# Windowed attention and a maxout layer on one core: scores of a batch's first chunk packed into six PSUM banks, the sinks' v product moved, one cast moved

## The chip, the cores and the metric

The kernel runs on one core of a Trainium2 chip. The metric is the device time of one execution in microseconds (us). All inputs come from the chip's memory (HBM) in float32, and the float32 output goes back there. Inside, the products run on bfloat16 with float32 sums.

The engines go by the names of the profile: PE is TensorE (PEld its weight loads), DVE is VectorE, ACT is ScalarE, POOL is GpSimd, SP is SyncE, which issues most transfers. Each engine takes its instructions strictly in the order in which the program emits them, and waits where the next one's operands or its buffer aren't ready.

## The reference

Two steps follow each other: an attention with a window and four sink positions, for 4 batches, 8 heads, 768 positions and a head size of 64; and a feed-forward layer whose hidden value is the larger of three products.

```python
scores = scale * np.matmul(q, k.transpose(0, 1, 3, 2))
is_sink = pos[None, :] < int(n_sink)             # n_sink = 4
in_window = (rel >= 0) & (rel < int(window))     # rel = query - key, window = 128
scores = np.where(is_sink | in_window, scores, -1000000000.0)
a = np.exp(scores - np.max(scores, axis=-1, keepdims=True))
a = a / (np.sum(a, axis=-1, keepdims=True) + 1e-09)
attn = np.matmul(a, v)
x = attn.transpose(0, 2, 1, 3).reshape(B * S, H * D)      # 3072 x 512
h = np.maximum(np.maximum(x @ w1, x @ w2), x @ w3)        # 512 -> 768
out = h @ w_out                                           # 768 -> 512
```

## The kernel before

**Tiling.** A batch's 768 positions are three *chunks* of 256, so there are twelve chunks, 0 to 11 (`NCH`), three to a batch (`CPB`). A chunk has two blocks of 128 queries, and its 8 heads are four *pairs* (`NP`): a = 0 and 1 are the two heads of a pair, whose 64 rows of head size lie on the upper and lower half of the 128 partitions, so that two matmuls of 64 rows stand side by side in TensorE.

**Scores.** `score(ci, pairs)` (L263) makes, transposed (keys on partitions), the score blocks that the window reaches. They have slots s of 128 columns in one bank of PSUM per head: s = 0 is the previous chunk's second key block against the first query block, s = 1 and 2 (one matmul of 256 columns) the chunk's first key block against both query blocks, s = 3 the second key block against the second. A batch's first chunk (ci % 3 == 0) has no previous one, so its slot 0 is empty: per head a matmul of 256 and one of 128 columns, in a bank of which three quarters are used. `expo` (L286) takes the exponential on ScalarE, one instruction per head (512 columns, or 384 in a first chunk); `mask` (L293) multiplies the pair by a 0/1 mask on VectorE (`msk`, in first chunks `msk0`; 1024 or 768 columns).

**Sinks.** The four sink positions lie in a batch's first chunk. `sink_k` (L229, GpSimd) gathers their keys, `sink_v` (L314) their values by eight small matmuls with a selection matrix (output `sv`), which VectorE copies to `vs`. Chunks 1 and 2 of a batch use them: `sink_score` (L298) makes the sink scores `sk`, ScalarE their exponential `e_sink`, and `av_open` (L328) starts the output `o` with the product of `e_sink` and `vs`. `av(ci, p)` (L343) then adds the window's blocks for one pair; VectorE takes the reciprocal `rc` of the sum of weights and writes `x_sb`.

**Feed-forward.** `xpose` (by TensorE and a copy) or `xpose_dma` (L379, by a DMA transpose on the SP queue) turns `x_sb` into `xT`. `ffn_h(ci, fp, wi)` (L386) multiplies by a third of the columns of w1, w2 or w3 (eight matmuls of 256 columns into one bank `h_ps`); for w1 ScalarE copies the result to `h_sb`, for the other two VectorE takes the maximum with it (L405). `ffn_y(ci, t)` (L409) makes one of a chunk's two output blocks from `h_sb` (six matmuls of 512 columns, `y_ps`), which ScalarE or VectorE copies to `y_sb` (L417).

**Stages.** From chunk 4 on a loop (L666) runs one stage per chunk n = i + 1: its attention, `ffn_y` of chunk i − 1 and `ffn_h` of chunk i, so each stage starts with scores, two `ffn_y`, then nine `ffn_h` with the four `av` between. The order within a stage is written out by hand: one for n = 4 (L668), one for the last two, one for the second and third chunks of a batch (L766: 5, 7, 8, 10) and one for the first chunks (L809: 6 and 9). In a stage for a first chunk the scores of pairs 0, 3 and 1 come before the two `ffn_y`, those of pair 2 after them. Before the loop chunks 0 to 3 have an order of their own; the part with chunk 3 ends at L660.

**Banks and queues.** PSUM has eight banks, which `bank()` hands out first in, first out, in the order of the program: a bank that was given back last comes last. The loads of q, k and v of chunk i + 3 and the transposes of kT, qT and xT are on the SP queue, in the order of the program. GpSimd makes most casts to bfloat16: `cast_qk` (L95) and `cast_v` (L105), the latter in four quarters per chunk.

Of the kernel before, what the change touches and what calls it, by code (L numbers as in the profile page):

```python
# [9 lines left out]
F32 = mybir.dt.float32  # L10
BF16 = mybir.dt.bfloat16
AF = mybir.ActivationFunctionType
# [4 lines left out]
def kernel(  # L17
# [13 lines left out]
    nc = tc.nc  # L31
# [8 lines left out]
    scale = 1.0 / (D ** 0.5)  # L40
    NP = H // 2
    CPB = S // 256
# [6 lines left out]
    with tc.manual_schedule():  # L49
        const = tc.alloc_tile_pool(name="const", bufs=1)  # L50
        raw = tc.alloc_tile_pool(name="raw", bufs=2)
        work = tc.alloc_tile_pool(name="work", bufs=2)
# [4 lines left out]
        def bank(shape, dtype, name):  # L57
            j = free.pop(0)
            x = psum.tile(shape, dtype, tag=f"b{j}", name=name)
            home[id(x)] = x, j  # L60
            return x

        def give(*banks):
            for x in banks:
                free.append(home.pop(id(x))[1])

        RING = 4
# [37 lines left out]
        def cast_v(ci, n, i, eng):  # L105
            if ci >= NCH:
                return
            eng.tensor_copy(  # L108
                vb[ci % RING][64 * i:64 * i + 64, n, :, 0:D],
                raws[ci, "v"][64 * n:64 * n + 64, :, i])  # L110

# [99 lines left out]
        def masks_late():  # L211
            for a in range(2):
                nc.gpsimd.tensor_scalar(msk[:, a], addm, 2.0 ** -30, 1.0, op0=ALU.mult, op1=ALU.add)
            for a in range(2):
                nc.gpsimd.tensor_scalar(msk0[:, a], addm0, 2.0 ** -30, 1.0, op0=ALU.mult, op1=ALU.add)

        sel = const.tile([128, 2, 32], BF16, name="sel")

        def sink_init():
# [43 lines left out]
        def score(ci, pairs):  # L263
# [3 lines left out]
            for p in pairs:  # L267
# [15 lines left out]
                e = work.tile([128, 2, 4, 128], BF16, tag="e", bufs=2 * NP, name="e_sb")  # L283
                es[ci, p] = e, st

        def expo(ci, p):  # L286
            lo = 0 if ci % CPB else 1
            e, st = es[ci, p]
            for a in range(2):
                nc.scalar.activation(e[:, a, lo:], st[a][:, lo:], AF.Exp, scale=scale)  # L290
                give(st[a])

        def mask(ci, p, eng=None):  # L293
            lo = 0 if ci % CPB else 1
            e = es[ci, p][0]
            (eng or nc.vector).tensor_mul(e[:, :, lo:], e[:, :, lo:], msk0 if lo else msk)  # L296
# [17 lines left out]
        def sink_v(b):  # L314

            x = vb[(b * CPB) % RING]
            sv = bank([128, 2, D + 1], F32, "sv")
            for a in range(2):
                for p in range(NP):
                    nc.tensor.matmul(  # L320
                        sv[32 * p:32 * p + 32, a], lhsT=sel[:, a], rhs=x[:, 0, 2 * p + a],
                        start=True, stop=True, tile_position=(0, 32 * p))
            nc.vector.tensor_copy(vs[b % 2], sv)
            give(sv)
# [18 lines left out]
        def av(ci, p):  # L343
            b, c = divmod(ci, CPB)
            o = os_[ci, p]
            e = es[ci, p][0]
            first = c == 0
            for t in range(2):
                for a in range(2):
                    blocks = [(1, ci, 0)] if t == 0 else [(2, ci, 0), (3, ci, 1)]  # L350
                    if t == 0 and c:
                        blocks = [(0, ci - 1, 1)] + blocks
                    for s, cv, n in blocks:
                        nc.tensor.matmul(  # L354
                            o[:, t, a], lhsT=e[:, a, s], rhs=vb[cv % RING][:, n, 2 * p + a],
                            start=first, stop=True, skip_group_check=True)
                        first = False
            rc = work.tile([128, 2, 2], F32, tag="rc", bufs=4, name="rc")
            nc.vector.reciprocal(rc, o[:, :, :, D])  # L359
            if ci not in xs:  # L360
                xs[ci] = work.tile([128, 2, NP, 2, D], BF16, tag="x", bufs=2, name="x_sb")
            nc.vector.tensor_mul(xs[ci][:, :, p], o[:, :, :, 0:D],  # L362
                                 rc.unsqueeze(3).to_broadcast([128, 2, 2, D]))
            give(o)
# [280 lines left out]
        load(5, 'v', gate=after(0))  # L645
        ffn_h(2, 0, 2)
        av(3, 0)
        cast_v(4, 0, 1, nc.vector)
        cast_v(4, 1, 0, nc.gpsimd)
        load(5, 'q')  # L650
        av(3, 2)
# [9 lines left out]
        def sinks(n):  # L661
            if n % CPB == 1:
                sink_k(n // CPB)
                sink_v(n // CPB)

        for i in range(3, NCH):  # L666
            n, m = i + 1, i - 1
            if i == 3:  # L668
# [17 lines left out]
                mask(n, 1)  # L686
                expo(n, 2)
                mask(n, 0)
                sink_score(n)
                ffn_h(i, 0, 0)  # L690
                expo(n, 3)
# [74 lines left out]
            elif n % CPB:  # L766
                load(i + 3)
                sink_score(n)
                score(n, (0,))
                expo(n, 0)  # L770
                score(n, (3,))
# [36 lines left out]
                ffn_h(i, 2, 2, 1 if i + 2 < NCH else 2)  # L808
            else:  # L809
                sink_k(n // CPB)  # L810
                sink_v(n // CPB)
                load(i + 3)
                score(n, (0,))
                expo(n, 0)
                score(n, (3,))
                score(n, (1,))
                expo(n, 1)
                expo(n, 3)
                ffn_y(m, 0, nc.vector)
                mask(n, 0)  # L820
                ffn_y(m, 1)
                score(n, (2,))
                mask(n, 3)
                av_open(n)
                mask(n, 1)
                expo(n, 2)
                av(n, 0)
                mask(n, 2)
                ffn_h(i, 1, 0)
                ffn_h(i, 0, 0)  # L830
                av(n, 1)
# [64 lines left out]
```

## Time and profile before

| | before |
|---|---|
| three runs, us | 178.89 to 179.43, median 179.43 |
| profiled execution, us | 179.04 |
| its span, first to last instruction, us | 177.3 |
| mean granted TensorE clock | 0.996 |
| busy, us: PE | 170.1 |
| busy, us: DVE | 126.5 |
| busy, us: ACT | 85.8 |
| busy, us: POOL | 67.1 |

A row of the timeline shows the start of a group of like instructions in us from the start of the span, its length, engine, line, operation, `output<-input`, the shape and the count; in brackets stands how long the engine had been idle before, and what ended that. Matmuls are pipelined: one of 128 columns shows a duration of some 0.2 us, but the next one starts long before its end, so the places of TensorE are read by starts. A row of a table by stretches has the stretch, its length, the busy time (and the count of instructions), the granted clock, the busy share of the DMA engines and GB/s.

### The profile page before, as it was taken

What the parts mean: (1) busy time and instruction counts of PE and PEld (TensorE: products, weight loads), DVE (VectorE), ACT (ScalarE), POOL (GpSimd) and SP (SyncE); (2) the same over time, 40 slices, a digit from 0 to 9 for tenths busy, and PEclk for the clock granted to TensorE, in tenths of its full rate; (3) what the DMA queues carried; (4) which work ended last, traced back from release to release, by engine and by line L of the source; (5) the groups of instructions that cost most, each with busy time, mean ns of one, the idle gap of its engine ahead of it and who ended that gap; (6) DMA issues with size and microseconds to landing.
All of it is one profiled execution on the core that took longest, in us unless ns stands there. A gap on an engine that the chain in (4) does not pass through costs nothing.

```text
span 177.3 us, 4632 instructions
## 1 busy us (share of the span) xinstructions
PE 170.1 (96%) x1872; PEld 127.1 (72%) x1872; DVE 126.5 (71%) x267; ACT 85.8 (48%) x171; POOL 67.1 (38%) x123
## 2 busy tenths in 40 slices
PE   6899999999998999999999999999999999999991
PEld 2446889856895597697696696796795895796870
DVE  3389738699698578796884984975885875966451
ACT  3498732577924822913724814814616617320210
POOL 6884344146580274544724624417427000000000
PEclk9999999999999999999999999999999999999998
DMA  5999999995999969999999999999999519305203
GB/s 141 290 287 203 224 248 259 216 265 148 290 140 236 94 142 299 129 245 173 251 269 189 210 301 160 213 303 153 198 293 198 150 34 379 125 11 170 120 0 118
DMA packets 69573, 34.90 MB, mean 197 GB/s; under 512 B 26544, under 2 KB 68016, under 8 KB 69552
## 3 DMA queue, kind: packets, MB, share of 16 engines
q1 hardware_dynamic: 64912, 31.33, 81.3%
q0 software_dynamic: 4496, 3.15, 11.6%
q8 instruction: 14, 0.23, 0.5%
q10 hardware_dynamic: 144, 0.13, 0.2%
q14 instruction: 7, 0.06, 0.1%
HBM read 25.17 MB, written 6.29 MB: 177 GB/s over the span
## 4 chain that ended last, share of the span: by engine, by line
PE 87%; DMA 4%; DVE 3%; SPq 2%; POOL 1%; ACT 1%; issue 0%; POOLq 0%
PE h_ps L394 52%; PE y_ps L415 18%; PE o L354 6%; PE st L278 6%; DMA q_raw<-in_q_dram 4%; SPq L90 2%; DVE h_sb L405 1%; PE o L336 1%; PE sk L304 1%; PE pt L118 1%; PE y_ps L425 1%; DVE x_sb L362 1%; POOL q_bf L102 1%; PE xt L375 1%; DVE vb L108 0%
## 5 line engine op out<-in xcount | busy, mean ns | idle before, releaser
L394 PE MATMUL h_ps<-xT,w 128*128 128x256 bf16 x864 | 100.7, 273 | 0.1
L394 PEld LDWEIGHTS <-w 128*128 128x128 bf16 x864 | 82.2, 98 | 10.4 <-issue 0.5
L405 DVE TENSOR_TENSOR h_sb<-h_sb,h_ps 128x512 bf16<-128x512 bf16 (+1 forms) x74 | 49.2, 671 | 21.2 <-PE h_ps L394 19.4
L290 ACT ACTIVATE e_sb<-st 128x512 bf16<-128x512 f32 (+1 forms) x96 | 46.6, 579 | 5.9 <-PE st L278 5.8
L401 ACT CAST h_sb<-h_ps 128x512 bf16<-128x512 f32 x36 | 21.2, 588 | 43.1 <-PE h_ps L394 42.9
L108 POOL CAST vb<-v_raw 64x512 bf16<-64x512 f32 x38 | 28.0, 737 | 15.8 <-DMA v_raw<-in_v_dram 14.5
L296 DVE TENSOR_TENSOR e_sb<-e_sb,msk 128x1024 bf16<-128x1024 bf16 (+1 forms) x42 | 31.6, 786 | 2.5 <-ACT e_sb L290 2.3
L415 PE MATMUL y_ps<-wo,h_sb 128*128 128x512 bf16 x138 | 32.4, 379 | 0.2 <-DVE h_sb L405 0.2
L415 PEld LDWEIGHTS <-h_sb 128*128 128x128 bf16 x138 | 12.6, 98 | 14.8 <-issue 1.6
L362 DVE TENSOR_TENSOR x_sb<-o,rc 128x256 bf16<-128x256 f32 x48 | 20.4, 425 | 1.6
L102 POOL CAST k_bf<-k_raw 128x512 bf16<-128x512 f32 x17 | 10.3, 625 | 28.5 <-DMA k_raw<-in_k_dram 28.5
L102 POOL CAST q_bf<-q_raw 128x512 bf16<-128x512 f32 x21 | 13.3, 658 | 16.4 <-DMA q_raw<-in_q_dram 13.0
L417 DVE COPY y_sb<-y_ps 128x512 f32<-128x512 f32 x13 | 9.0, 691 | 13.7 <-PE y_ps L415 13.7
L354 PE MATMUL o<-vb,e_sb 128*128 128x65 bf16 x352 | 16.5, 193 | 0.0
L354 PEld LDWEIGHTS <-e_sb 128*128 128x128 bf16 x352 | 14.6, 97 | 2.0 <-DVE e_sb L296 0.2
L278 PE MATMUL st<-qT,kT 64*128 64x128 bf16 (+1 forms) x256 | 14.5, 238 | 0.5 <-ACT kT L125 0.5
L278 PEld LDWEIGHTS <-kT 64*128 64x128 bf16 x256 | 8.1, 94 | 7.1 <-issue 4.9
L310 ACT ACTIVATE e_sink<-sk 128x256 bf16<-128x256 f32 x8 | 3.1, 385 | 14.8 <-PE sk L304 14.8
L359 DVE RECIPROCAL rc<-o 128x4 f32<-128x4 f32 x48 | 8.4, 175 | 1.3 <-PE o L354 1.0
L417 ACT COPY y_sb<-y_ps 128x512 f32<-128x512 f32 x10 | 5.9, 586 | 3.3 <-PE y_ps L415 2.7
L102 ACT CAST k_bf<-k_raw 128x512 bf16<-128x512 f32 x5 | 3.1, 626 | 6.5 <-DMA k_raw<-in_k_dram 6.5
L180 PE MATMUL warm<-wz 128*128 128x512 bf16 x14 | 4.5, 462 | 1.2 <-DVE wz L169 1.2
(69 smaller groups left out, 72.7 us busy)
## 6 DMA issues: line engine op xcount, KB each, us to landing
k_raw<-in_k_dram SPq DMA_DIRECT2D x12, 512.0 KB, 5.5
q_raw<-in_q_dram SPq DMA_DIRECT2D x12, 512.0 KB, 7.0
v_raw<-in_v_dram SPq DMA_DIRECT2D x12, 512.0 KB, 8.2
out_dram<-y_sb SPq DMA_DIRECT2D x11, 512.0 KB, 4.0
w<-in_moe_w_dram POOLq DMA_DIRECT2D x5, 256.0 KB, 8.7
w<-in_moe_w_dram POOLq DMA_DIRECT2D x2, 512.0 KB, 9.8
wo<-in_moe_w_out_dram POOLq DMA_DIRECT2D x2, 384.0 KB, 9.8
kT<-k_bf SPq DMA_TRANSPOSE x16, 3.7
```

Of the source, the lines that this page charges most:

```text
L102: f(x[:, 2 * g:2 * g + 2].rearrange("q p i a d -> q p a i d"), y[:, 4 * g:4 * g + 4].rearrange("q (p a) i d -> q p a i d", a=2))
L108: eng.tensor_copy(vb[ci % RING][64 * i:64 * i + 64, n, :, 0:D], raws[ci, "v"][64 * n:64 * n + 64, :, i])
L278: nc.tensor.matmul(st[a][:, s:s + q1 - q0].rearrange("q n (i r) -> q n i r", i=2), lhsT=x[hp, n, p].rearrange("q i r -> q (i r)"), rhs=qc[ ...
L290: nc.scalar.activation(e[:, a, lo:], st[a][:, lo:], AF.Exp, scale=scale)
L296: (eng or nc.vector).tensor_mul(e[:, :, lo:], e[:, :, lo:], msk0 if lo else msk)
L354: nc.tensor.matmul(o[:, t, a], lhsT=e[:, a, s], rhs=vb[cv % RING][:, n, 2 * p + a], start=first, stop=True, skip_group_check=True)
L362: nc.vector.tensor_mul(xs[ci][:, :, p], o[:, :, :, 0:D], rc.unsqueeze(3).to_broadcast([128, 2, 2, D]))
L394: nc.tensor.matmul(hp[:, f].rearrange("q (i t r) -> q i t r", i=2, t=2), lhsT=w_sb[wi][:, ds, c0:c0 + 128], rhs=xTs[ci][:, :, ds].rearrang ...
L401: nc.scalar.copy(dst, hp)
L405: nc.vector.tensor_max(dst[:, x], dst[:, x], hp[:, x])
L415: nc.tensor.matmul(yp, lhsT=hs[ci][:, fb, t * 128:(t + 1) * 128], rhs=wo[:, fb], start=(fb == 0), stop=(fb == FB - 1))
L417: (nc.scalar.copy if eng is None else eng.tensor_copy)(ys[ci][:, t], yp)
```

## The change

Three edits.

*Packed scores.* In the stages of chunks 6 and 9 the scores go to three pairs of banks, all four slots of each used: the first pair of banks holds pair 0 and the last block of pair 2, the next one pair 1 and the last block of pair 3, the third the rest of pairs 2 and 3. All sixteen matmuls come in one row ahead of the two `ffn_y`. There are six exponentials of 512 columns where there were eight of 384, and three masks of 1024 columns where there were four of 768. `av` finds its weights through `weight()`. The packed masks `mskp` are made once, by four copies on ScalarE, in the part with chunk 3.

*Sinks' v product.* `sink_v` leaves the head of the stages 4, 6 and 9. For batch 1 it stands right before `sink_score(4)`, after two masks; for batches 2 and 3 it comes one stage later, in those of chunks 7 and 10, right after `sink_score`.

*One cast.* The quarter of chunk 4's V that VectorE cast in the part with chunk 3 is cast by ScalarE.

```diff
@@ cast_v
-            eng.tensor_copy(
+            (eng.copy if eng is nc.scalar else eng.tensor_copy)(
                 vb[ci % RING][64 * i:64 * i + 64, n, :, 0:D],
                 raws[ci, "v"][64 * n:64 * n + 64, :, i])
@@ new
+        mskp = const.tile([128, 2, 2, 4, 128], BF16, name="mskp")
+        def masks_packed():
+            nc.scalar.copy(mskp[:, 0, :, 0:3], msk0)
+            nc.scalar.copy(mskp[:, 0, :, 3:4], msk0[:, :, 2:3])
+            for j in range(2):
+                nc.scalar.copy(mskp[:, 1, :, 2 * j:2 * j + 2], msk0[:, :, 0:2])
@@ new
+        PLAN = (((0, 1, 0), (0, 3, 2), (2, 3, 3)), ((1, 1, 0), (1, 3, 2), (3, 3, 3)), ((2, 1, 0), (3, 1, 2)))
+        unit = {(p, s + x): (j, u + x) for j in range(3) for p, s, u in PLAN[j]
+                for x in range(2 if s == 1 else 1)}
+        packed = {}
+        def score_packed(ci, j):
+            st = [bank([128, 4, 128], F32, "st") for a in range(2)]
+            for p, s, u in PLAN[j]:
+                n, q0, w = (0, 0, 2) if s == 1 else (1, 1, 1)
+                for a in range(2):
+                    hp = slice(64 * a, 64 * a + 64)
+                    nc.tensor.matmul(
+                        st[a][:, u:u + w].rearrange("q n (i r) -> q n i r", i=2),
+                        lhsT=kT[ci % RING][hp, n, p].rearrange("q i r -> q (i r)"),
+                        rhs=qT[ci % RING][hp, p, :, q0:q0 + w].rearrange("q i n r -> q n i r"),
+                        start=True, stop=True)
+            e = work.tile([128, 2, 4, 128], BF16, tag="e", bufs=2 * NP, name="e_sb")
+            packed[ci, j] = e, st
+        def expo_packed(ci, j):
+            e, st = packed[ci, j]
+            for a in range(2):
+                nc.scalar.activation(e[:, a], st[a], AF.Exp, scale=scale)
+                give(st[a])
+        def mask_packed(ci, j):
+            e = packed[ci, j][0]
+            nc.vector.tensor_mul(e, e, mskp[:, j // 2])
+        def weight(ci, p, a, s):
+            if (ci, 0) in packed:
+                j, u = unit[p, s]
+                return packed[ci, j][0][:, a, u]
+            return es[ci, p][0][:, a, s]
@@ av
-                            o[:, t, a], lhsT=e[:, a, s], rhs=vb[cv % RING][:, n, 2 * p + a],
+                            o[:, t, a], lhsT=weight(ci, p, a, s), rhs=vb[cv % RING][:, n, 2 * p + a],
@@ part with chunk 3
         av(3, 0)
-        cast_v(4, 0, 1, nc.vector)
+        cast_v(4, 0, 1, nc.scalar)
+        masks_packed()
@@ sinks, at the head of the stage of chunk 4
                 sink_k(n // CPB)
-                sink_v(n // CPB)
@@ stage of chunk 4
                 mask(n, 1)
                 expo(n, 2)
                 mask(n, 0)
+                sink_v(n // CPB)
                 sink_score(n)
                 ffn_h(i, 0, 0)
@@ stages of chunks 5, 7, 8, 10
                 load(i + 3)
                 sink_score(n)
+                sink_v(n // CPB) if n % CPB == 1 else None
                 score(n, (0,))
@@ stages of chunks 6 and 9
                 sink_k(n // CPB)
-                sink_v(n // CPB)
                 load(i + 3)
-                score(n, (0,))
-                expo(n, 0)
-                score(n, (3,))
-                score(n, (1,))
-                expo(n, 1)
-                expo(n, 3)
+                score_packed(n, 0)
+                expo_packed(n, 0)
+                score_packed(n, 1)
+                expo_packed(n, 1)
+                score_packed(n, 2)
+                mask_packed(n, 0)
                 ffn_y(m, 0, nc.vector)
-                mask(n, 0)
+                expo_packed(n, 2)
                 ffn_y(m, 1)
-                score(n, (2,))
-                mask(n, 3)
+                mask_packed(n, 1)
                 av_open(n)
-                mask(n, 1)
-                expo(n, 2)
                 av(n, 0)
-                mask(n, 2)
+                mask_packed(n, 2)
                 ffn_h(i, 1, 0)
```

1 line of the change is left out of this document (removed).

## The prediction

> **What bounds the kernel.** I read first the chain that ended last, then the busy time of TensorE (PE) by stretches.
>
> ```profile
> PE 87%; DMA 4%; DVE 3%; SPq 2%; POOL 1%; ACT 1%; issue 0%; POOLq 0%
> ```
> ```profile
> 51.00:58.00 7.00, 6.30 (x78) 1.00 0.88 203
> 58.00:160.00 102.00, 101.97 (x1157) 1.00 0.96 196
> ```
>
> PE carries 87% of the chain. From 58 to 160 us it is busy for 101.97 of 102.00 us, at full granted clock (1.00). So an edit pays there only if it shortens the row of matmuls itself, and any wait that it adds is paid in full. Just before, from 51 to 58 us, PE is idle for 0.70 us; there VectorE (DVE) is read next, around the V cast that the change takes off it.
>
> ```profile
> 52.42 0.42 DVE L362 TENSOR_TENSOR x_sb<-o,rc 128x256 bf16<-128x256 f32 x1
> 52.88 0.68 DVE L108 CAST vb<-v_raw 64x512 bf16<-64x512 f32 x1
> 53.59 0.18 DVE L359 RECIPROCAL rc<-o 128x4 f32<-128x4 f32 x1
> 53.81 0.43 DVE L362 TENSOR_TENSOR x_sb<-o,rc 128x256 bf16<-128x256 f32 x1
> 54.15 0.17 DVE L359 RECIPROCAL rc<-o 128x4 f32<-128x4 f32 x1
> 54.35 0.42 DVE L362 TENSOR_TENSOR x_sb<-o,rc 128x256 bf16<-128x256 f32 x1
> 54.70 1.87 DVE L405 TENSOR_TENSOR h_sb<-h_sb,h_ps 128x512 bf16<-128x512 bf16 x3
> 56.48 0.42 DVE L376 COPY xT<-xt 128x512 bf16<-128x512 bf16 x1
> 56.82 0.28 DVE L323 CAST vs<-sv 128x130 bf16<-128x130 f32 x1
> 58.12 0.69 DVE L417 COPY y_sb<-y_ps 128x512 f32<-128x512 f32 x1 [1.01 <-PE y_ps L415]
> 58.72 1.28 DVE L296 TENSOR_TENSOR e_sb<-e_sb,msk 128x1024 bf16<-128x1024 bf16 x2
> 61.47 1.05 DVE L296 TENSOR_TENSOR e_sb<-e_sb,msk 128x1024 bf16<-128x1024 bf16 x1 [1.47 <-ACT e_sb L290]
> ```
> ```profile
> 56.62 1.46 PE L415 MATMUL y_ps<-wo,h_sb 128*128 128x512 bf16 x6 [0.22 <-DVE h_sb L405]
> 58.01 0.62 PE L278 MATMUL st<-qT,kT 64*128 64x128 bf16 x12
> 58.55 0.29 PE L304 MATMUL sk<-qT,ks 128*32 128x256 bf16 x4
> 58.78 1.05 PE L394 MATMUL h_ps<-xT,w 128*128 128x256 bf16 x8
> 59.86 0.29 PE L336 MATMUL o<-vs,e_sink 32*128 32x130 bf16 x8
> ```
>
> DVE has no gap up to 57.1 us. Its last `h_sb` ends at 54.70 + 1.87 = 56.57, and `ffn_y(2, 0)` starts 0.05 later, at 56.62: VectorE is the bound of this one place.
>
> **1. The V cast, chunk 4 (once).** `x_sb` ends at 52.42 + 0.42 = 52.84, and `rc` follows at 53.59 because the cast stands between. Without it `rc` follows as the next one does (54.15, which is 0.09 before the end 53.81 + 0.43 = 54.24), at 52.75: DVE is 0.84 us earlier. The last `h_sb` then ends at 55.73 and `y_ps` can start at 55.78. PE is there by then: the last `x_sb` (54.35 + 0.42) moves to 53.93, before PE ends its `h_ps`, so transposes and twelve scores run without their waits.
>
> On ScalarE the cast and the four copies of `masks_packed` cost nothing:
>
> ```profile
> 55.48 0.58 ACT L376 COPY xT<-xt 128x512 bf16<-128x512 bf16 x1 [5.59 <-PE xt L375]
> 55.96 2.07 ACT L290 ACTIVATE e_sb<-st 128x512 bf16<-128x512 f32 x4
> 58.44 1.08 ACT L290 ACTIVATE e_sb<-st 128x512 bf16<-128x512 f32 x2 [0.40 <-PE st L278]
> 59.41 0.39 ACT L310 ACTIVATE e_sink<-sk 128x256 bf16<-128x256 f32 x1
> ```
>
> ScalarE (ACT) idles 5.59 us there, some 5.0 when PE's transposes come earlier. The added work is about 2,560 columns: five pieces, at the copy's 0.58 for 512, make 2.9 us; as steps of a row of exponentials ((2.07 − 0.60)/3 = 0.49) they make 2.5. The data is there: GpSimd has cast the other quarters of that V before. No row shows a copy of ScalarE from SBUF of that kind, but twice the cost would only just use up the cover; past it each 1 us more would hold the `xT` copy and the exponentials by as much.
>
> **2. The sinks' v product in the same stage.** Its 8 matmuls leave the front of the stage (they take part of the time in which `y_ps` waits anyway) and stand before `sink_score`. They cost about 0.08 us there: 0.18 in the first row of the next part (82.61 to 82.79), less 0.1 for a change of matmul shape, which they share with `sink_score`. But `vs` is now copied by VectorE behind `mask(4, 1)` and `mask(4, 0)`, and `av_open(4)` needs it: a new wait. Moved by 0.84, the masks end at 58.72 + 1.28 − 0.84 = 59.16, `vs` starts 0.09 before that and ends 0.28 later, at 59.35; the sink product `o` can start at 59.40. Without this wait it would start at 59.86 − 0.84 = 59.02. So 0.38 is lost, and 0.46 is left of 0.84. Behind the waiting `o` stand, on PE, `ffn_y(2, 1)` and everything later.
>
> The next thing PE meets is the transposed `xT` of chunk 4, needed one stage on:
>
> ```profile
> 64.65 0.53 SPq L90 DMA_DIRECT2D v_raw<-in_v_dram  x1
> 67.71 2.06 SPq L381 DMA_TRANSPOSE xT<-x_sb  x1
> ```
> ```profile
> DMA to landing us min/median/max: 5.8/5.8/5.8
> ```
> ```profile
> 73.94 0.27 PE L394 MATMUL h_ps<-xT,w 128*128 128x256 bf16 x1
> ```
>
> Issued at 67.71, it lands 5.8 us later, at 73.5, and is used at 73.94: 0.4 us of slack. On the SP queue it stands behind the load of chunk 6's V (64.65), which PE doesn't hurry. I take its landing as standing still: with 0.05 from landing to start, PE can be at most 0.36 us earlier here. Between 0.36 and 0.46 I take **0.36**; ends kept: 0 (it lands 0.4 later) and 0.46.
>
> **3. Packed scores, chunks 6 and 9 (twice).**
>
> ```profile
> 82.61 0.25 PE L320 MATMUL sv<-vb,sel 128*32 128x65 bf16 x8
> 82.79 0.67 PE L278 MATMUL st<-qT,kT 64*128 64x256 bf16 x12
> 83.46 2.75 PE L415 MATMUL y_ps<-wo,h_sb 128*128 128x512 bf16 x12
> 86.14 0.34 PE L278 MATMUL st<-qT,kT 64*128 64x256 bf16 x4
> 86.42 0.35 PE L354 MATMUL o<-vb,e_sb 128*128 128x65 bf16 x6
> ```
> ```profile
> 81.92 1.49 DVE L405 TENSOR_TENSOR h_sb<-h_sb,h_ps 128x512 bf16<-128x512 bf16 x2 [0.25 <-PE h_ps L394]
> ```
>
> The matmuls stay sixteen, of the same widths. `y_ps` starts at 83.46, 0.05 after the last `h_sb` (81.92 + 1.49 = 83.41), on which it depends: that floor stays. Sixteen scores in the place of product and twelve start at 82.61 and need 12 in about 0.62 (0.67 with some waiting) and four more in 0.16, with the change of shape: 83.4. So they fit ahead of the floor, and `y_ps` still starts at 83.46. Its twelve matmuls at 0.215 end at 86.05, and now `o` follows at once. How that looks without scores between, another place shows:
>
> ```profile
> 39.90 1.46 PE L415 MATMUL y_ps<-wo,h_sb 128*128 128x512 bf16 x6
> 41.20 0.41 PE L354 MATMUL o<-vb,e_sb 128*128 128x65 bf16 x8
> ```
>
> Six `y_ps` take 1.30 from start to `o`, so twelve take 2.60 (or 2.59), where 86.42 − 83.46 = 2.96 are paid now. Gain **0.37** each. Only 0.16 of it is the scores themselves; the rest is two changes of matmul shape (128 rows to 64 and back).
>
> What must be ready: the first packed mask by 86.0. Six exponentials of 512 columns replace eight of 384, 0.49 each from about 83.1 (the first six scores, from 82.61, end near 83.0): the first pair ends near 84.2, its mask at 84.9 or, at the long 1.05, 85.3. It stands ahead of the `y_sb` copy, which needs `y_ps` at 84.9 and loses at most 0.4, hidden, since its bank is wanted at 86.2. Six banks are in use and the two `y_ps` take the last two; all were released before 83.46. The stage has one mask less, so VectorE gets freer. No edit issues a transfer or moves one on a queue; the order on SP is as before.
>
> **4. The v product in chunks 7 and 10 (twice).** It stands between two groups of the shapes of its neighbours and costs 0.08. It also takes a bank: banks go round first in, first out, so the last pair before `y_ps` now needs, for its second half, the bank of the last `h_ps`, where `y_ps` had it before.
>
> ```profile
> 94.42 1.49 DVE L405 TENSOR_TENSOR h_sb<-h_sb,h_ps 128x512 bf16<-128x512 bf16 x2 [0.25 <-PE h_ps L394]
> ```
> ```profile
> 95.34 0.84 PE L278 MATMUL st<-qT,kT 64*128 64x128 bf16 x18
> 96.11 0.60 PE L415 MATMUL y_ps<-wo,h_sb 128*128 128x512 bf16 x2
> ```
>
> That bank is free at 94.42 + 1.49 = 95.91, usable at 95.96. Eighteen scores take 95.34 to 96.11 with 0.11 for the change of shape, so a pair takes 0.22; the last one from 95.96 ends at 96.29, or 96.27 with unrounded starts. Loss **0.17** each (0.08 if the wait is covered).
>
> **The sum.** −0.36 − 2 × 0.37 + 2 × 0.17 = −0.76 us. The profiled execution took 179.04 us (span 177.3 and 1.7 around it): 178.28. It lies 0.39 below the median of the three runs, 179.43; the mean of the four executions is 179.2. From that I forecast **178.4 us**, between 178.28 and 178.67 by the two bases.
>
> **Rivals.** (A) *The transfer decides chunk 4.* If the queue lands `xT` 0.4 later in most executions, part 1 gives nothing: −0.40, 178.8. For it: 0.4 us of slack behind 5.8 of flight. Chance 0.18.
> (B) *The bank wait is covered and `xT` isn't met:* −0.46 − 0.74 + 0.16 = −1.04, 178.2. Against it: the order of the banks. Chance 0.10.
> (C) *Slower: the packed mask takes the place of the second visit.* If the first mask waits for all six exponentials, not its own two, it starts at 86.1 and, at 1.05, ends at 87.1; `o` starts at 87.15 instead of 86.42. That is +0.73 twice, −0.36 and +0.34: +1.44, 180.6. It decides from a mask that ends after 86.0. Against it: each pair has a tile and a wait of its own. Chance 0.09.
> (D) *The masks before `vs` run long.* The mask at 61.47 took 1.05 where two took 1.28 at 58.72; it ran while GpSimd cast:
>
> ```profile
> 60.81 1.18 POOL L102 CAST q_bf<-q_raw 128x512 bf16<-128x512 f32 x2 [7.54 <-DMA q_raw<-in_q_dram]
> ```
>
> Two masks at 1.05 end 0.8 later, the gain of chunk 4 turns into a loss of 0.35, and the sum is −0.05: 179.1. GpSimd idles there until 60.8, so `q_raw` would have to land 2 us sooner. Chance 0.04. The Trainium skill, page "SBUF — State Buffer", section "SBUF: two separate sides", says that a DVE operation with two SBUF inputs and a GpSimd operation that reads SBUF exclude each other for a whole instruction; the longer mask beside the cast agrees.
> (E) *Changing shape costs nothing,* so that a second visit is worth its four matmuls: −0.36 − 0.32 + 0.34 = −0.34, 178.9. The rows speak against it (0.37, not 0.16). Chance 0.03. This is what the Trainium skill gives, page "TensorE: Matmul & The Clock Gate", section "Back-to-back issue gap", where a gap follows from the columns alone; the rows decide.
>
> **The numbers.** The forecast has 0.56, most of it beyond 0.3% (0.54 us), which is about what a measurement of this kernel can tell from no change; of it 0.47 count as faster and 0.09 as within. With B faster is 0.57; A, D and E bring within to 0.34; C is slower, 0.09. The range, 177.8 to 179.4, takes in B from the lower base (178.0) and A from the upper (179.03), each with some 0.2 to 0.4 for the spread of the runs, and leaves out C.
>
> **What would show it.** Chunk 4: no cast on DVE near 52.9, `y_ps` near 55.8, the sink `o` near 59.4 with its weight load waiting for `vs`, the first `h_ps` of chunk 4 just behind the landing of `xT`. Chunks 6 and 9: sixteen scores in one row, 2.59 from `y_ps` to `o`. Chunks 7 and 10: the last pair of scores waiting for `h_sb`. It is wrong if `xT` lands with PE, if a packed mask comes after 86.0 on this clock, or if a transfer of a later chunk loses its slack.

## The result, and the profile after

| | before | after |
|---|---|---|
| median of six runs each, us | 179.42 (178.74 to 179.64) | 177.82 (177.62 to 178.16) |
| profiled execution, us | 179.04 | 177.77 |
| its span, us | 177.3 | 176.0 |

The ratio of the mean times is 0.9922, with a 95% interval of 0.9901 to 0.9942: some 1.4 us faster (1.0 to 1.8). The profiled executions differ by 1.27 us, where the forecast had a sum of 0.76.

The page of after, first line, busy time of the engines, and the shares of the chain that ended last:

```profile
span 176.0 us, 4619 instructions
...
PE 168.1 (96%) x1859; PEld 127.1 (72%) x1872; DVE 124.0 (70%) x264; ACT 88.3 (50%) x172; POOL 65.6 (37%) x123
...
PE 88%; DMA 4%; SPq 2%; DVE 1%; POOL 1%; issue 1%; POOLq 0%
```

VectorE's share of the chain falls from 3% to 1%, TensorE's rises from 87% to 88%. The chain is again almost all matmuls, and VectorE's one hold on it is smaller. To see where the time came from, I read the starts of TensorE stage by stage: each chunk's first and last `h_ps` ("h" and "e"), the first `y_ps` of `ffn_y(2, 0)` ("y") and the sink product `o` of chunk 4 ("os"). All other stages from chunk 2's first `h_ps` on agree within 0.05 us. "Second" is a further profiled execution of the same kernel. The trace of after lacks 13 of 150 records of `y_ps` matmuls, so rows of it below show x5 or x11 where 6 or 12 ran; the places are read by starts.

| us, from to | before | second before | after | second after |
|---|---|---|---|---|
| chunk 4, e2 to y | 2.53 | 2.06 | 1.20 | 1.33 |
| chunk 4, y to os | 3.23 | 3.23 | 3.74 | 3.64 |
| chunk 4, os to h4 | 14.08 | 14.07 | 14.08 | 14.08 |
| chunk 6, e4 to h5 | 4.20 | 4.19 | 3.76 | 3.76 |
| chunk 7, e5 to h6 | 4.70 | 4.70 | 4.86 | 4.86 |
| chunk 9, e7 to h8 | 4.19 | 4.20 | 3.75 | 3.75 |
| chunk 10, e8 to h9 | 4.70 | 4.70 | 4.87 | 4.87 |

Between the two profiles: −1.33 + 0.51 − 0.44 + 0.16 − 0.44 + 0.17, with 0.07 more before chunk 2's first `h_ps`, gives −1.30; the spans, unrounded, differ by 1.29 us. All that stands behind the start of chunk 4's `y_ps` adds up to almost nothing (0.51 − 0.88 + 0.33 = −0.04): what chunks 6 and 9 gain pays for the wait for `vs` and for chunks 7 and 10, and the span gets shorter by that one earlier start. The row e2 to y of before varies by 0.47 between two executions of one kernel, so what chunk 4 brings (−0.82 here, −0.32 between the second executions, where the start of the run brings another −0.80) is not one number.

The 0.47 lies on VectorE, as its rows in the second execution of before show:

```profile
49.22 1.91 DVE L296 TENSOR_TENSOR e_sb<-e_sb,msk 128x768 bf16<-128x768 bf16 x3
...
53.65 0.42 DVE L108 CAST vb<-v_raw 64x512 bf16<-64x512 f32 x1
```

In the first execution these three masks of chunk 3 took 2.32, and the cast took 0.68; it began while GpSimd cast keys (52.66 to 53.27), which it did not in the second. From the first mask to the next `h_sb` 2.24 us pass there and 2.01 here; the cast holds the queue for 0.84 there and for 0.57 here. Together that is 0.50. So the 0.84 of the prediction is the cast's price in one execution, not in every one.

Chunk 4 in the timeline of after, TensorE:

```profile
54.82 0.62 PE L287 MATMUL st<-qT,kT 64*128 64x128 bf16 x12
55.37 1.47 PE L459 MATMUL y_ps<-wo,h_sb 128*128 128x512 bf16 x5
...
59.10 0.29 PE L381 MATMUL o<-vs,e_sink 32*128 32x130 bf16 x8 [0.46 <-DVE vs L368]
```

And VectorE there:

```profile
53.95 1.87 DVE L449 TENSOR_TENSOR h_sb<-h_sb,h_ps 128x512 bf16<-128x512 bf16 x3
...
57.55 1.29 DVE L341 TENSOR_TENSOR e_sb<-e_sb,msk 128x1024 bf16<-128x1024 bf16 x2
58.76 0.29 DVE L368 CAST vs<-sv 128x130 bf16<-128x130 f32 x1
```

Two things are to be seen. The wait that was forecast is there: `o` stands 0.46 us for `vs`, which VectorE copies behind two masks. And one that was taken for a fixed floor is gone: the last `h_sb` ends at 53.95 + 1.87 = 55.82, but `y_ps` starts at 55.37, 0.45 *before* it. Before the change `y_ps` started 0.05 after it.

ScalarE in the same stretch:

```profile
49.99 0.62 ACT L108 CAST vb<-v_raw 64x512 bf16<-64x512 f32 x1
50.63 0.83 ACT L221 COPY mskp<-msk 128x768 bf16<-128x768 bf16 x1
51.37 0.40 ACT L222 COPY mskp<-msk 128x256 bf16<-128x256 bf16 x1
51.67 1.13 ACT L224 COPY mskp<-msk 128x512 bf16<-128x512 bf16 x2
54.97 0.59 ACT L420 COPY xT<-xt 128x512 bf16<-128x512 bf16 x1 [2.16 <-issue]
```

The five added pieces take from 49.99 to 51.67 + 1.13 = 52.80, 2.81 us (2.5 to 2.9 were forecast), and 2.16 us of idle time are left behind them: hidden, as forecast.

Chunk 6, TensorE and then VectorE:

```profile
81.86 0.83 PE L307 MATMUL st<-qT,kT 64*128 64x256 bf16 x16
82.63 2.76 PE L459 MATMUL y_ps<-wo,h_sb 128*128 128x512 bf16 x11
85.23 0.35 PE L398 MATMUL o<-vb,e_sb 128*128 128x65 bf16 x6
```
```profile
81.16 1.49 DVE L449 TENSOR_TENSOR h_sb<-h_sb,h_ps 128x512 bf16<-128x512 bf16 x2 [0.26 <-PE h_ps L438]
83.41 0.72 DVE L323 TENSOR_TENSOR e_sb<-e_sb,mskp 128x1024 bf16<-128x1024 bf16 x1 [0.75 <-ACT e_sb L318]
```

All sixteen scores stand in one row, 2.60 us pass from `y_ps` to `o` (2.59 forecast, 2.96 before), and the first packed mask ends at 84.13, 1.1 us before `o` needs it. Here too `y_ps` (82.63) starts ahead of the end of the last `h_sb` (81.16 + 1.49 = 82.65), if only by 0.02.

Chunk 7, TensorE and then VectorE:

```profile
94.03 0.24 PE L365 MATMUL sv<-vb,sel 128*32 128x65 bf16 x8
94.20 0.94 PE L287 MATMUL st<-qT,kT 64*128 64x128 bf16 x18
95.07 2.12 PE L459 MATMUL y_ps<-wo,h_sb 128*128 128x512 bf16 x8
```
```profile
93.22 1.49 DVE L449 TENSOR_TENSOR h_sb<-h_sb,h_ps 128x512 bf16<-128x512 bf16 x2 [0.26 <-PE h_ps L438]
```

The eighteen scores take 0.87 from start to `y_ps`, 0.77 before. With the 0.08 of the product that is the forecast loss of 0.17. The last `h_sb` ends at 94.71, where the forecast saw the last pair's bank come free.

### The profile page after: what moved, and what is told of

It reads as the page before. It is cut to its first block, busy times and chain, and to the rows that moved or that the text cites. A ratio compares the mean times of both kernels' runs of the same rounds, so it can differ in the third digit from the quotient of the medians.

```text
span 176.0 us, 4619 instructions
## 1 busy us (share of the span) xinstructions
PE 168.1 (96%) x1859; PEld 127.1 (72%) x1872; DVE 124.0 (70%) x264; ACT 88.3 (50%) x172; POOL 65.6 (37%) x123
## 4 chain that ended last, share of the span: by engine, by line
PE 88%; DMA 4%; SPq 2%; DVE 1%; POOL 1%; issue 1%; POOLq 0%
PE h_ps L438 53%; PE y_ps L459 17%; PE o L398 6%; PE st L287 5%; DMA q_raw<-in_q_dram 4%; SPq L90 2%; PE xt L419 1%; PE o L381 1%; PE pt L118 1%; PE sk L349 1%; PE st L307 1%; PE y_ps L469 1%; DVE e_sb L341 1%; POOL q_bf L102 1%; DVE y_sb L461 0%
## 5 line engine op out<-in xcount | busy, mean ns | idle before, releaser
L335 ACT ACTIVATE e_sb<-st 128x512 bf16<-128x512 f32 (+1 forms) x80 | 39.9, 593 | 0.5 <-PE st L287 0.4
L108 POOL CAST vb<-v_raw 64x512 bf16<-64x512 f32 x38 | 26.3, 692 | 15.8 <-DMA v_raw<-in_v_dram 11.7
L459 PE MATMUL y_ps<-wo,h_sb 128*128 128x512 bf16 x125 | 31.5, 380 | 0.6
L341 DVE TENSOR_TENSOR e_sb<-e_sb,msk 128x1024 bf16<-128x1024 bf16 (+1 forms) x34 | 25.1, 773 | 2.3 <-ACT e_sb L335 2.1
L287 PE MATMUL st<-qT,kT 64*128 64x128 bf16 (+1 forms) x224 | 12.5, 237 | 0.5 <-ACT kT L125 0.5
L287 PEld LDWEIGHTS <-kT 64*128 64x128 bf16 x224 | 7.1, 94 | 6.0 <-issue 3.8
L318 ACT ACTIVATE e_sb<-st 128x512 bf16<-128x512 f32 x12 | 6.1, 613 | 4.7 <-PE st L307 4.7
```

The costliest lines, as they stand in the source:

```text
L108: (eng.copy if eng is nc.scalar else eng.tensor_copy)(vb[ci % RING][64 * i:64 * i + 64, n, :, 0:D], raws[ci, "v"][64 * n:64 * n + 64, :, i])
L287: nc.tensor.matmul(st[a][:, s:s + q1 - q0].rearrange("q n (i r) -> q n i r", i=2), lhsT=x[hp, n, p].rearrange("q i r -> q (i r)"), rhs=qc[ ...
L459: nc.tensor.matmul(yp, lhsT=hs[ci][:, fb, t * 128:(t + 1) * 128], rhs=wo[:, fb], start=(fb == 0), stop=(fb == FB - 1))
```

## The experiments

**Theory 1 (banks).** Before, `y_ps` did not wait for the last `h_sb` as data; only its fifth and sixth matmuls read that block. It waited for a *bank*: the one that the last `h_ps` had used, given back by the same VectorE instruction. `sv` took one bank at the head of the stage, so the count came out that way; without it the first `y_ps` gets a bank given back earlier. A timeline row names the releasing instruction, which is the same for both reasons. **Theory 2 (the prediction's floor).** `y_ps` waits for the last `h_sb` as data, so its start is fixed by VectorE, and the larger gain came from a luckier `xT` landing.

### The parts alone

*The cast alone* (before, with the cast on ScalarE):

```diff
         av(3, 0)
-        cast_v(4, 0, 1, nc.vector)
+        cast_v(4, 0, 1, nc.scalar)
         cast_v(4, 1, 0, nc.gpsimd)
```

> The kernel before with one edit: the quarter of chunk 4's V is cast on ScalarE, nothing else. VectorE's queue gets 0.84 us shorter (0.68 of cast and the overlaps lost on both its sides). If that queue is what holds ffn_y(2, 0), as the prediction said, it starts 0.84 earlier, and the sink product of chunk 4 too, since vs is copied long before: about -0.84 in all. If xT of chunk 4 stands still at 73.5 us (rival A and the bound that the forecast took), no more than -0.36.

Measured: 178.70 us, ratio 0.9976 (0.9957 to 0.9995), 0.4 us faster. In the profile e2 to y falls by 0.60 against one execution of before, by 0.13 against the other, and chunk 6 loses 0.16, although no edit touches it. The size expected for a queue that holds `ffn_y(2, 0)`, −0.84, doesn't show: `y_ps` still waits for VectorE, but the three masks ahead took 2.57 here (2.32 and 1.91 before), and from the first of them to the next `h_sb` 2.49 us pass (2.24 and 2.01). That gives back 0.25 of the cast's 0.84, or 0.48 of its 0.57. `xT` (landed at 73.48, used at 73.81) held nothing up. The loss at chunk 6 has its own cause. VectorE and GpSimd in this kernel:

```profile
85.44 0.95 DVE L296 TENSOR_TENSOR e_sb<-e_sb,msk 128x768 bf16<-128x768 bf16 x1
```
```profile
85.37 0.61 POOL L108 CAST vb<-v_raw 64x512 bf16<-64x512 f32 x1
```

The same two rows of before, VectorE and GpSimd:

```profile
85.56 0.66 DVE L296 TENSOR_TENSOR e_sb<-e_sb,msk 128x768 bf16<-128x768 bf16 x1
```
```profile
85.20 0.61 POOL L108 CAST vb<-v_raw 64x512 bf16<-64x512 f32 x1
```

The cast that the mask meets ends at 85.37 + 0.61 = 85.98 here and at 85.81 before, and the mask ends at 86.39 and 86.22: 0.41 behind the end of the cast in both. So how long a mask takes depends on how much of a cast is still to run when it begins. `o` waits for that mask and starts at 86.45. The place of GpSimd's casts relative to TensorE shifts with every change, by a tenth or two.

*The sinks' v product alone* (before, with its three moves):

```diff
@@ sinks, at the head of the stage of chunk 4
                 sink_k(n // CPB)
-                sink_v(n // CPB)
@@ stage of chunk 4
                 mask(n, 0)
+                sink_v(n // CPB)
                 sink_score(n)
@@ stages of chunks 5, 7, 8, 10
                 sink_score(n)
+                sink_v(n // CPB) if n % CPB == 1 else None
@@ stages of chunks 6 and 9
                 sink_k(n // CPB)
-                sink_v(n // CPB)
```

> The kernel before with the sinks' v product moved as in the change, nothing else. Theory 1, formed from the two traces (the first ffn_y waits for the bank of the last h_ps, and its own data is needed only by its fifth matmul; without the v product ahead it gets an older bank): chunks 6 and 9 -0.25 each though their scores are as before, chunks 7 and 10 +0.17 each, chunk 4 -0.25 (ffn_y 0.74 earlier, 0.5 lost again at vs): -0.4 in all. Theory 2, the prediction's floor (ffn_y waits for the last h_sb as its data): 0 in chunks 6 and 9, +0.17 in 7 and 10, +0.49 in chunk 4 because vs comes behind two masks: +0.8 in all.

Measured: 179.34 us, ratio 1.0001 (0.9983 to 1.0020). Neither size came out; the starts decide. TensorE at chunk 4 and chunk 6:

```profile
56.20 1.46 PE L415 MATMUL y_ps<-wo,h_sb 128*128 128x512 bf16 x6
...
83.20 2.76 PE L415 MATMUL y_ps<-wo,h_sb 128*128 128x512 bf16 x12
```

VectorE at chunk 4:

```profile
54.87 1.87 DVE L405 TENSOR_TENSOR h_sb<-h_sb,h_ps 128x512 bf16<-128x512 bf16 x3
```

`y_ps` starts at 56.20, 0.54 before the last `h_sb` ends (56.74), with the cast still on VectorE: theory 2's floor isn't there. What this part brings it gives back. By stages: e2 to y −0.62 against the first profile of before, y to os +0.41 (the wait for `vs`), chunks 7 and 10 +0.16 and +0.17, chunk 9 −0.22, and chunk 6 only −0.06, as a mask there took 0.97 and again ended 0.41 behind a cast of GpSimd.

*The packed scores alone* (after, with cast and product put back):

```diff
-        cast_v(4, 0, 1, nc.scalar)
+        cast_v(4, 0, 1, nc.vector)
         masks_packed()
@@ and sink_v back at the heads of the stages 4, 6 and 9
```

> The kernel before with the scores of chunks 6 and 9 packed (and the masks for it made on ScalarE), nothing else. Sixteen scores follow the v product; by both theories ffn_y starts about 0.1 later than before (TensorE itself, no longer the bank), and the output product follows it directly, 2.59 after its start instead of 2.96: -0.27 each, -0.54 in all. If only the columns of matmuls counted and a change of shape nothing, -0.1 at most.

Measured: 178.66 us, ratio 0.9960 (0.9948 to 0.9973), 0.7 us faster. Chunks 6 and 9 give −0.26 each: with `sv` at the head `y_ps` still has the late bank, and only the second visit to the scores is saved. The other 0.18 of after's 0.44 come with the move of `sv`. This profile also holds 0.52 us of loss in os to h4, which is taken up below.

*Before once more*, for a second profile of it:

> The kernel before once more, for a second profile. If xT of chunk 4 lands when the queue of transfers lets it, whatever the engines do, it lands at 73.5 again within 0.3 us. If it varies from execution to execution, it lands up to 2 us apart, as it did between the profiles of before (73.5) and after (71.6).

Measured: 179.56 us in one execution, with e2 to y at 2.06 and `xT` of chunk 4 landing at 73.96, 0.43 later than in the first; TensorE is 0.51 later there too.

### The banks turned by one

After, with the list of free banks turned by one ahead of the scores of chunks 4, 6 and 9. No instruction is added or removed; only which bank goes to whom.

```diff
+        def turn_banks():
+            free.append(free.pop(0))
@@ stage of chunk 4
                 load(i + 3)
+                turn_banks()
                 score(n, (0, 1))
@@ stages of chunks 6 and 9
                 load(i + 3)
+                turn_banks()
                 score_packed(n, 0)
```

> The changed kernel, with the list of free banks turned by one place ahead of the scores of chunks 4, 6 and 9 and no instruction added, so that the first ffn_y of these stages gets the bank of the last h_ps, as before the change. Theory 1 (the bank): ffn_y(2, 0) starts at about 55.9 instead of 55.4, chunk 4 loses 0.5 in all; chunks 6 and 9 lose 0.08 each: +0.66 against the changed kernel. Theory 2 (the data of the last h_sb): no difference.

Measured: 178.82 us, ratio 0.9984 (0.9968 to 1.0001), against 0.9943 (0.9924 to 0.9962) for after in the same series: about 0.8 us slower. TensorE at chunks 4 and 6:

```profile
56.34 1.46 PE L462 MATMUL y_ps<-wo,h_sb 128*128 128x512 bf16 x6 [0.22 <-DVE h_sb L452]
...
82.73 0.83 PE L310 MATMUL st<-qT,kT 64*128 64x256 bf16 x16
83.58 2.75 PE L462 MATMUL y_ps<-wo,h_sb 128*128 128x512 bf16 x12
```

VectorE at chunk 4:

```profile
54.41 1.87 DVE L452 TENSOR_TENSOR h_sb<-h_sb,h_ps 128x512 bf16<-128x512 bf16 x3
```

`y_ps` is back at 0.06 behind the last `h_sb` (56.28), with before's `[0.22 <-DVE h_sb]`. By stages e2 to y is 0.60 longer than in the second profile of after, chunks 6 and 9 0.07 each, chunk 10 0.06: 0.80. The data are the same in both kernels, so it was the bank. Counted through the program, the first `y_ps` of chunks 4, 6 and 9 gets the bank of the last `h_ps` in before and with the banks turned, and that of the last but one in after. Theory 1 is shown, theory 2 falls.

After was run beside it, and once more in the next series:

> The changed kernel once more, beside the next three on one chip: some -1.3 to -1.6 us against before. Its xT of chunk 4 lands at 71.6 again if the change itself brings that forward, elsewhere between 71 and 74 if executions differ.

> The changed kernel a third time, on one chip with the next two: -1.0 to -1.6 us against before. In an execution in which xT of chunk 4 lands after 73.2 us, about 0.5 of that is missing, as in the profiles of the packed scores alone and of the late third group.

178.02 and 177.88 us, ratios 0.9943 (0.9924 to 0.9962) and 0.9924 (0.9903 to 0.9944): the gain stands in each. `xT` of chunk 4 landed at 72.18 and 72.44: executions differ, and in neither did it hold TensorE.

### What a second visit to the scores costs

After, with the third packed group behind the two `ffn_y`:

```diff
-                score_packed(n, 2)
                 mask_packed(n, 0)
                 ffn_y(m, 0, nc.vector)
-                expo_packed(n, 2)
                 ffn_y(m, 1)
+                score_packed(n, 2)
+                expo_packed(n, 2)
```

> The changed kernel, with the third packed group of scores (four matmuls of 256 columns) behind the two ffn_y again: packed, but not in a row. If the gain comes from two changes of matmul shape, each of these stages loses 0.19: +0.4 against the changed kernel. If it comes from the packing (fewer exponentials and masks), no difference; if from the scores' own columns, none either, since they are only moved.

Measured: 178.49 us, ratio 0.9973 (0.9957 to 0.9990). TensorE at chunk 6:

```profile
82.51 0.62 PE L307 MATMUL st<-qT,kT 64*128 64x256 bf16 x12
83.06 2.76 PE L459 MATMUL y_ps<-wo,h_sb 128*128 128x512 bf16 x12
85.75 0.39 PE L307 MATMUL st<-qT,kT 64*128 64x256 bf16 x4
86.08 0.35 PE L398 MATMUL o<-vb,e_sb 128*128 128x65 bf16 x6
```

From `y_ps` to `o` 3.02 us pass, 0.42 more than in after, and the row of scores ahead of `y_ps` (82.51 to 83.06) only 0.22 shorter than after's 0.77: chunks 6 and 9 are 0.21 and 0.22 longer. So the same four scores cost 0.42 behind `y_ps` and 0.22 in the row, with no wait of TensorE there, and the 0.2 between is put down to the two changes of matmul shape. That bears out the prediction's 0.21 for the changes, but the scores themselves are worth 0.2 and not 0.16: by these figures a second visit is half change, half scores. The Trainium skill, page "TensorEngine Tiling (Array Packing)", section "Key Properties", says that a change of the tiling mode drains TensorE; it gives no time, and this trace puts it at about 0.1 us a change.

### The wait for `vs`

After, with product and sink scores of chunk 4 ahead of masks and third exponential, so that neither `vs` nor `e_sink` is late:

```diff
                 score(n, (2, 3))
+                sink_v(n // CPB)
+                sink_score(n)
                 mask(n, 1)
                 expo(n, 2)
                 mask(n, 0)
-                sink_v(n // CPB)
-                sink_score(n)
```

> The changed kernel, with sink_v and sink_score of chunk 4 emitted ahead of its first two masks and of the third exponential, so that vs and e_sink come first on VectorE and ScalarE; TensorE's order is the same. If the sink product waits for vs behind the masks, it starts at about 58.6 instead of 59.1: -0.5 against the changed kernel. If that wait was covered by something else, no difference.

Measured: 177.91 us, ratio 0.9935 (0.9916 to 0.9954), not to be told from after beside it (0.9943). TensorE:

```profile
58.85 0.33 PE L381 MATMUL o<-vs,e_sink 32*128 32x130 bf16 x8
59.41 1.46 PE L459 MATMUL y_ps<-wo,h_sb 128*128 128x512 bf16 x6 [0.22 <-ACT e_sb L335]
```

y to os falls by 0.44, but the next row gives most of it back: `ffn_y(2, 1)` now waits for the bank of a score that ScalarE's later exponential releases (0.31 in os to h4). One wait had another behind it. So only the product was moved:

```diff
                 score(n, (2, 3))
+                sink_v(n // CPB)
                 mask(n, 1)
                 expo(n, 2)
                 mask(n, 0)
-                sink_v(n // CPB)
                 sink_score(n)
```

> The changed kernel, with only sink_v of chunk 4 emitted ahead of its first two masks, so that the copy to vs comes right behind the y_sb copy on VectorE; sink_score and the exponentials stay where the change has them. The sink product then waits for e_sink instead of vs, 0.3 us earlier (3.3 us behind ffn_y instead of 3.65), and ffn_y(2, 1) finds the bank of e_sink, not that of the third exponential, on which the run with both moved lost what it had won: -0.3 us against the changed kernel, as far as its transfer of xT lets it. If the place is bounded by something else, no difference.

Measured: 177.92 us, ratio 0.9939 (0.9916 to 0.9962; after beside it 0.9924). TensorE:

```profile
59.33 0.29 PE L381 MATMUL o<-vs,e_sink 32*128 32x130 bf16 x8 [0.16 <-ACT e_sink L355]
```

`o` waits 0.16 for `e_sink` instead of 0.46 for `vs`, y to os falls to 3.43, and nothing behind it is late. The times, 177.35 to 179.20, spread too far to show 0.2 to 0.3 us.

### The bank of chunks 7 and 10

The kernel with only the product of chunk 4 moved up, and with the sinks' scores and v product of chunks 7 and 10 in one bank; ScalarE makes both the exponential and the copy to `vs`:

```diff
+        def sink_both(ci):
...
+            both = bank([128, 512], F32, "skv")
+            st = both[:, 0:256].rearrange("q (n k) -> q n k", n=2)
+            sv = both[:, 256:256 + 2 * (D + 1)].rearrange("q (a d) -> q a d", a=2)
...
+            nc.scalar.activation(e, st, AF.Exp, scale=scale)
+            nc.scalar.copy(vs[b % 2], sv)
+            give(both)
@@ stages of chunks 5, 7, 8, 10
-                sink_score(n)
-                sink_v(n // CPB) if n % CPB == 1 else None
+                (sink_both if n % CPB == 1 else sink_score)(n)
```

> The run before it, with the sinks' scores and v product of chunks 7 and 10 in one bank (v product first, and vs copied by ScalarE behind e_sink), so that they take one bank and not two. If the loss in these stages is half a wait for the bank of the last h_ps, the distance from the last h_ps of one chunk to the first of the next falls from 4.87 to 4.78 us, twice; if it is only the matmuls of the product, it stays. Rival: the copy on ScalarE delays its six exponentials by 0.2 us and a mask comes late.

Measured: 178.23 us, ratio 0.9942 (0.9920 to 0.9964). TensorE at chunk 7:

```profile
95.43 0.84 PE L287 MATMUL st<-qT,kT 64*128 64x128 bf16 x18
96.19 2.12 PE L482 MATMUL y_ps<-wo,h_sb 128*128 128x512 bf16 x9
```

The eighteen scores are back at 0.76, and the two stages at 4.79 and 4.76 (4.86 each before this edit, 4.70 without the product): about half of the loss there was the bank, the rest the product's own 0.08. No mask comes late: TensorE waits for none. The time doesn't show it, since this profile too has 0.56 us in os to h4.

### When `xT` of chunk 4 lands

Three profiles (packed scores alone, third group late, one bank) have that loss. TensorE and SP's queue with the packed scores alone:

```profile
74.23 1.03 PE L438 MATMUL h_ps<-xT,w 128*128 128x256 bf16 x8 [0.36 <-DMA xT<-x_sb]
```
```profile
65.27 0.55 SPq L90 DMA_DIRECT2D v_raw<-in_v_dram  x1
67.29 4.19 SPq L425 DMA_TRANSPOSE xT<-x_sb  x1
```

That is rival A: `h_ps` starts 0.04 after `xT` lands at 74.19. In after it lands at 71.60, and `h_ps` starts at 73.18 without a wait. In the thirteen traces that keep the queue's order it landed between 71.60 and 74.36, always 0.84 to 0.85 us behind V of chunk 6, which is issued ahead of it. So, in the version with the earlier product, V of chunk 6 was put behind it:

```diff
-                load(i + 3)
+                load(i + 3, 'kq')
@@ the four casts of that V go with it
                 xpose_dma(n)
+                load(i + 3, 'v')
+                cast_v(i + 3, 0, 0, nc.gpsimd)
...
                 turn_dma(i + 3, 'k')
```

> The kernel with only the sinks' v product of chunk 4 ahead of its masks, and with one more edit: V of chunk 6 is issued on SP's queue behind the transposing transfer of chunk 4 (x_sb to xT) instead of ahead of it, and cast after that. In all runs so far that transfer landed 0.85 us behind V of chunk 6 (71.7 and 72.6 in the kernel named, 73.3 and 74.2 where only the packed scores were changed), although it is issued at about 67. Theory 1 (it lands late because V's transfer is ahead of it): it lands at 70.5 to 72 in every execution, the first ffn_h of chunk 4 starts 14.08 us after the sinks' product of that chunk and waits for no transfer; the slow end of the times (178.8 to 179.2) goes, the median falls 0.1 to 0.3 us. Theory 2 (the landing is set by how long any transfer of that stretch takes, whatever stands ahead): it still lands between 71.6 and 74.4, the times spread as before. Price of the edit by either: K and Q of chunk 7 and the turns of chunk 6 stand behind V, V is cast some 5 us later, and nothing on TensorE waits for it.

Measured: 177.64 us (177.45 to 177.76), ratio 0.9912 (0.9892 to 0.9933). SP's queue, and the landing of `xT`:

```profile
67.21 1.81 SPq L425 DMA_TRANSPOSE xT<-x_sb  x1
69.11 0.53 SPq L90 DMA_DIRECT2D v_raw<-in_v_dram  x1
```
```profile
DMA to landing us min/median/max: 3.2/3.2/3.2
```

It lands at 70.36, 1.2 us earlier than in any other trace, after 3.2 us of flight (5.8 in before). Os to h4 is 14.08, and from 46 us on TensorE's list of waits is empty. So the landing was set by V ahead of it, and theory 2 of this run falls. The six times lie within 0.31 us, where twelve of the version it was made from lay within 1.85; three of those twelve lay above 178.8, so six without such a one can still be chance. The Trainium skill, page "DMA: Bandwidth & Descriptors", section "Queues, rings and completion order", says that a transfer's semaphore counts up only after every earlier write of the same DMA engine; the constant 0.84 agrees.

This is the lowest median of all kernels run, but its interval overlaps after's, so that it beats after isn't shown. It would keep more distance from rival A.

## Why the prediction came out as it did

The direction was right, the size too small: −0.76 forecast, −1.3 between the profiled executions, −1.4 (−1.0 to −1.8) in the times. That 177.82 lies within the range at all, 0.02 above its lower end, is luck in part: the range reached down there for rival B, of which one half came (`xT` not met) and the other didn't (the bank wait of chunks 7 and 10 covered); what filled the place was an error that no rival named.

| term, us | forecast | between the first profiles |
|---|---|---|
| chunk 4, start of `y_ps` | −0.84 | −1.33 |
| chunk 4, new wait for `vs` | +0.38 | +0.51 |
| chunk 4, cap by `xT` | +0.10 | 0 |
| chunks 6 and 9, each | −0.37 | −0.44 |
| chunks 7 and 10, each | +0.17 | +0.16, +0.17 |
| start of the run | 0 | +0.07 |

**The step that failed** is the floor: "0.05 after the last `h_sb` (81.92 + 1.49 = 83.41), on which it depends: that floor stays", said of `y_ps` in chunks 6 and 9, and in chunk 4 the same reading, by which `y_ps` can start at 55.78 and no sooner. The start of `y_ps` 0.05 behind the last `h_sb` was read as data; it was a bank, and the edit that takes `sv` from the head of the stage changes who gets which bank. At chunk 4 this is the larger part of the missing gain: with the cast gone, VectorE ends its last `h_sb` at 55.82, so by the floor `y_ps` would start at 55.87; it starts at 55.37, 0.50 earlier. At chunks 6 and 9 it is 0.07 each, as the turned banks show. The prediction had applied the bank order in chunks 7 and 10, where it cost time, and got 0.17 right to 0.01; it didn't ask the same question where a bank came free.

**The cap by `xT`** was taken as a landing that stands still at 73.5. It moved to 71.6, because V of chunk 6 ahead of it moved; so the 0.46 wasn't cut to 0.36. In other executions the cap is real, so the step was wrong in its certainty rather than in its mechanism. Whether rival A decides changes from one execution to the next.

**The new wait** had the right place and mechanism; 0.38 was the size with the floor, and as `y_ps` starts earlier by more, VectorE is later by more beside it: 0.46 of waiting in the row, 0.51 in the stage.

**Packed scores**: 2.60 from `y_ps` to `o`, 2.59 forecast. Rival C is out (the mask has 1.1 us to spare), and so is E: the four scores cost 0.2 us more as a second visit behind `ffn_y` than in the row. Rival B's covered bank wait didn't come: with one bank less, half of the loss went.

**Rival D** had the right mechanism in another place: the masks before `vs` took 1.29 for two, as forecast, but masks of chunk 6 ran long in two of the single parts.

Cast and product alone give −0.4 and 0.0, the packed scores −0.7, the whole −1.4. The parts add up to −1.1, and as each is known to 0.2 to 0.4 us, the times can't tell that from the whole. By stages, the sinks' move costs in chunks 7 and 10 what it brings in chunks 6 and 9: with packed scores alone chunks 6 and 7 together take 3.94 + 4.70 = 8.64 us, with the whole change 3.76 + 4.86 = 8.62. Its profit is at chunk 4, and there in part only, as long as `vs` is waited for.

**What stays open.** Why V of chunk 6, and `xT` behind it, land at one of two times isn't settled. It is set by 61 us already: Q of chunk 5, issued at 53 to 54 us in all traces, took 5.7 to 6.1 us in eight of the fourteen (all three of after among them) and 7.1 to 7.7 in the other six, both of before among these. All four traces with `sv` at the heads of the stages have the longer one, and eight of the ten with it moved the shorter, so the change may well have a part in it; but it doesn't decide it alone: the kernel with the third group late differs from after only from 82 us on, and its transfer took 7.7. The trace with V behind `xT` has the shorter flight (6.05), so what that order does in the longer one was seen only through the narrow spread of its times.

## What to carry to other kernels

When a matmul starts just behind the instruction that makes its input, ask first which of its matmuls reads that input, and which bank it writes to: the same instruction may release both, and only moving the banks tells them apart. An edit that takes one buffer from a ring shifts every later user by one place, so count the ring for each stage that is touched, where it helps as well as where it hurts. Before a landing is taken as fixed, look at what is issued ahead of it on the same queue.

## What the runs showed of the hardware

- A change of matmul shape on TensorE costs some 0.1 us: 0.21 and 0.22 for two of them.
- A mask on VectorE that begins inside a GpSimd cast of V, with 0.16 us or more of the cast left, ended 0.40 to 0.41 us behind the end of that cast in all 45 cases with 768 columns and 0.54 in all but eight of 133 with 1024, over the fourteen traces (0.58 to 0.97 and 0.70 to 1.14 long by how much of the cast was left; 0.55 and 0.68 without a cast). In those eight, mask and cast began within 0.01 us of each other; the mask took 0.68 as alone, and the cast 1.16 in place of 0.61. This is what the Trainium skill, page "SBUF — State Buffer", section "SBUF: two separate sides", calls an exclusive lock for a whole instruction; the trace agrees.
- A transposing transfer of x landed 0.84 to 0.85 us behind the 512 KB load ahead of it, in all thirteen traces; without that load ahead it took 3.2 us instead of 4.6 to 6.9. The last one (issued at 157 to 159 us), with no load ahead either, took 3.0 to 3.1 in all fourteen.
- ScalarE copies from SBUF to SBUF took 0.83, 0.61 and 0.40 us for 768, 512 and 256 columns of bfloat16.
